# Two units of weights on GpSimd's queue and another order of the head's steps, in linear attention followed by a gated feed-forward layer

## The chip, the cores and the metric

The kernel runs on one core of one Trainium2 chip. The metric is device time in microseconds from launch to end, lower is better. A profiled execution gives besides a span, from the first to the last instruction of the core, and a trace of every engine. TensorE (PE) multiplies; VectorE (DVE), ScalarE (ACT) and GpSimd (POOL) work elementwise; SyncE (SP) issues most of the DMA transfers.

## The reference

There are 8 batches of 8 heads, 576 tokens and head size 64. For each head the kernel computes a small matrix from keys and values, applies it to the queries, and normalises each row. The rows of all heads of one token are then put side by side (512 wide) and go through a feed-forward layer with a sigmoid gate, whose weights come as 64-bit floats:

```python
kv = einsum('bhsd,bhse->bhde', k, v)            # 64 x 64 per head
o  = einsum('bhsd,bhde->bhse', q, kv)
o  = o / sqrt(mean(o*o, axis=-1) + 1e-6) * g_norm
x  = o.transpose(0, 2, 1, 3).reshape(4608, 512)
gate = 1 / (1 + exp(-(x @ w_gate)))             # w_gate, w_val: 512 x 1536
out  = (gate * (x @ w_val)) @ w_out             # w_out: 1536 x 512
```

## The kernel before

The 4608 tokens are worked in nine groups of 512. Group 0 is computed plainly; groups 1 to 8 use products of sums of blocks, a scheme of fast matrix multiplication with 26 products in place of 32. The change touches only the head: the attention of the first two batches (eight pairs of heads, n = 0 to 7), the conversion of the first five units of weights, and the first four blocks of group 0's first layer.

**A pair of heads** goes through eleven steps (`attention`, L265 to L345). KV (TensorE) forms both 64x64 matrices; KVO (DVE) copies them to SBUF and issues the loads of k and v for pair n+4. Q (TensorE) turns the queries; QO (ACT) copies them and issues the load of q for pair n+4. U (TensorE) multiplies the two. SQ (ACT) squares, SUM (DVE) adds up, ROOT (ACT) takes the root, NORM (DVE: a reciprocal and a product) scales. X (TensorE) turns the rows to columns and XO (ACT) copies them to xT, the operand of the feed-forward layer. KV and Q of a pair share one place in PSUM, so KVO waits for both, QO waits for KVO, and the next pair's KV waits for QO. U and X of a pair share another, one for even and one for odd pairs.

**A unit of weights** is 128 columns of w_gate and the same of w_val (2 x 512 KB of 64-bit floats). `load_unit` (L135) loads it with two transfers into one of three staging buffers, and `convert` (L161) makes 32-bit floats from it in five steps on DVE (c0 to c4) with two on ACT between (a0 follows c0, a1 follows c1, c2 waits for a0, c3 for a1). Unit u+3 goes into the buffer that c4 of unit u has freed.

**A block** (`Plain`, L554) is one 128-column piece of both products for group 0: four accumulating matmuls for the gate, four for the value, each over 128 of the 512 inputs and all 512 tokens. Block f needs unit f converted, and matmul m of it needs XO of pair m. Blocks 0 to 2 share two PSUM banks. CG and CV copy a finished block out, G is its sigmoid straight from PSUM, S the sigmoid of a copy, M and E form the product of gate and value.

**The order** is written out by hand as a string of tokens (L594): `KV0` is the step KV of pair 0, `c1.2` step c2 of unit 1, `a1.0` its step a0, `b0.1.3` matmul 3 of the value of block 0, `w2` the loads of unit 2, and `warm10` ten matmuls of the identity that only keep TensorE busy. Each engine runs its own instructions in this order and waits only where an operand or a place needs it. SyncE's queue is in the order in which the program issues loads: k, v and q of pairs 0 and 1, unit 0, pairs 2 and 3 (L231), and then as the tokens come. SyncE has at most eight transfers in flight: each issue waits for the one eight before it.

After the head TensorE goes on with blocks 4 to 11 (`plain`, L573), in which DVE converts the other units step by step. After block 8 the keys and values of batch 2 are multiplied (L366), and then GpSimd begins to form the sums of weights for the fast scheme (L741). Until then it has nothing to do but the identity matrix at the start (`make_identity`, L252).

Of the kernel before, what the change touches and what calls it, by code (L numbers as in the profile page):

```python
# [20 lines left out]
def kernel(  # L21
# [11 lines left out]
    nc = tc.nc  # L33
# [26 lines left out]
    NMT = DM // P  # L60
# [74 lines left out]
    def load_unit(u):  # L135
        if u >= len(units):
            return
        kind, f = units[u]
        staged[u] = st = raw.tile([P, 2, DM], I64, tag="st", name="st", bufs=NST)
        for i in range(2):  # L140
            if kind == "gv":
                src = (moe_w_gate, moe_w_val)[i].rearrange("(m p) f -> p m f", p=P)[:, :, P * f:P * f + P]
                nc.sync.dma_start(out=st[:, i].rearrange("p (m f) -> p m f", m=NMT), in_=src)
            else:
                nc.sync.dma_start(out=st[:, i], in_=moe_w_out[P * (f + i):P * (f + i) + P, :])

# [14 lines left out]
    def convert(u):  # L161
# [45 lines left out]
        def s4():  # L207

            m, p = d["m"], d["p"].bitcast(FP32)
            if kind == "gv":  # L210
                vec.scalar_tensor_tensor(out=m, in0=m, scalar=g_col, in1=p, op0=ALU.mult, op1=ALU.mult)
            else:
                vec.tensor_tensor(out=m, in0=m, in1=p, op=ALU.mult)
            if u > 1:
                load_unit(u + NST)
# [15 lines left out]
    for n in range(4):  # L231
        load_kv(n)
        load_q(n)
        if n == 1:
            load_unit(0)


    w1 = const.tile([P, N3, 4 * NMT, 2, P], FP32, name="w1")
    w2 = const.tile([P, NFT, DM], FP32, name="w2")
# [333 lines left out]
    def plain(c, u, ps):  # L573
# [18 lines left out]


    order = """  # L594
        warm10 KV0 Q0 KVO0 QO0 w1 warm3 U0 SQ0 KV1 SUM0 ROOT0 Q1 KVO1 NORM0 QO1 warm3 U1 SQ1 SUM1 X0 c0.0 c0.1
        XO0 ROOT1 NORM1 warm13 KV2 warm2 Q2 KVO2 a0.0 c0.2 X1 a0.1 c0.3 c0.4 QO2 w2 warm6 U2 SQ2 KV3 Q3 b0.0.0 b0.1.0
        KVO3 XO1 QO3 w3 U3 SUM2 KV4 Q4 ROOT2 NORM2 SQ3 SUM3 ROOT3 X2 XO2 b0.0.1 b0.1.1 b0.0.2 NORM3 X3 KVO4 QO4
        U4 c1.0 a1.0 c1.1 a1.1 c1.2 c1.3 b0.1.2 KV5 Q5 KVO5 XO3 b0.0.3 b0.1.3 SQ4 c1.4 w4 SUM4 QO5 U5 CG0 CV0
        KV6 Q6 b1.0.0 ROOT4 NORM4 X4 b1.1.0 b1.0.1 b1.1.1 SQ5 SUM5 ROOT5 KVO6 QO6 XO4 U6 NORM5 X5 c2.0 c2.1 a2.0
        c2.2 b1.0.2 KV7 Q7 SQ6 SUM6 a2.1 b1.1.2 ROOT6 c2.3 b1.0.3 XO5 b1.1.3 KVO7 QO7 U7 c2.4 NORM6 CG1 X6 CV1  # L600
        b2.0.0 SQ7 XO6 b2.1.0 b2.0.1 c3.0 SUM7 ROOT7 b2.1.1 c3.1 a3.0 a3.1 NORM7 X7 XO7 c3.2 c3.3 c3.4 b2.0.2
        b2.1.2 b2.0.3 c4.0 S0 S1 b2.1.3 M0 G2 M1 b3.0.0 b3.1.0 a4.0 E2 c4.1 a4.1 c4.2 c4.3 b3.0.1 b3.1.1 b3.0.2
        b3.1.2 b3.0.3 b3.1.3 c4.4
    """
    blks, copies = {}, {}
    warm = mm0_ps()
    for token in order.split():
        name = token.rstrip("0123456789.")
        n = [int(i) for i in token[len(name):].split(".")]
        f = n[0]  # L610
# [10 lines left out]
        elif name == "CG":  # L621
            copies[f, 0] = sg_tile()
            nc.scalar.copy(out=copies[f, 0], in_=blks[f].ps[0])
        elif name == "CV":
            copies[f, 1] = sg_tile()
            nc.vector.tensor_copy(out=copies[f, 1], in_=blks[f].ps[1])
        elif name == "S":
            nc.scalar.activation(out=copies[f, 0], in_=copies[f, 0], func=AF.Sigmoid)
        elif name == "M":
            nc.vector.tensor_tensor(out=gv_tile(0, F_ORDER[f]), in0=copies[f, 1], in1=copies[f, 0], op=ALU.mult)  # L630
        elif name == "G":
            blks[f].gate()
        elif name == "E":
            blks[f].end()
        elif name in ("c", "a"):
            conversion[f][name][n[1]]()
        elif name == "w":
            load_unit(f)
        elif name == "warm":
            for _ in range(f):  # L640
                nc.tensor.matmul(warm[:, 0:P], ident, ident, start=True, stop=True)
        else:
            a[f][steps[name]]()
            if token == f"Q{NE - 1}":
                first_ctx.__exit__(None, None, None)
                hp = ctx.enter_context(tc.tile_pool(name="hp", bufs=1))
                h_main = [hp.tile([P, 4 * NT, P], FP32, name=f"h{j}") for j in range(N3)]
                h_more = hp.tile([P, N3, 3 * NT, P], FP32, name="h_more")
# [449 lines left out]
    X1 = (12, 16, 16, 17, 18, 18, 19, 19, 19, 20, 20, 21, 21, 24, 25, 25, 25, 25)  # L1098
    X2 = (14, 15, 16, 17, 19, 21, 24, 25, 25, 25, 25, 25, 25, 25, 25, 25, 25, 25)
    X3 = (7, 8, 11, 11, 12, 13, 14, 14, 16, 16, 19, 22, 22, 22, 22, 22, 23, 23)  # L1100
# [49 lines left out]
```

## Time and profile before

| | |
|---|---|
| time, median of 3 runs | 1019.01 us (1017.05 to 1019.85) |
| profiled execution, its own time | 1019.05 us |
| its span | 1017.3 us |
| TensorE busy | 1005.9 us, 99% of the span |
| DVE, ACT, GpSimd busy | 728.1, 350.2, 602.4 us |
| moved by DMA | 193.89 MB, mean 191 GB/s |
| first weights converted (c4 of unit 0 starts) | 21.45 us |
| first matmul of block 0 starts | 22.85 us |
| keys and values of batch 2 (L366) start on TensorE | 98.34 us |
| first sum on GpSimd (L741) starts | 99.11 us |

Times in the views are in microseconds from the span's start. A line of the timeline gives start, length, engine, source line, operation, output<-input, shape, how many instructions are merged, and in brackets how long the engine was idle before and what released it. TensorE runs a 32-bit matmul in two recorded parts, so a count of 24 is twelve matmuls. A line of windows gives the stretch, the busy time of each engine with its count, the granted clock of TensorE, the mean busy share of the 16 DMA engines and what they moved in GB/s. Issuing a DMA isn't counted as busy.

### The profile page before, as it was taken

The numbers are of one execution on the slowest core, as the hardware profiler recorded it, in microseconds if no ns is written. First come the engines' busy times: TensorE is split into PE (matmuls) and PEld (weight loads), VectorE is DVE, ScalarE is ACT, GpSimd is POOL, SyncE is SP. The second block draws the span as 40 slices with busy tenths as digits, with TensorE's granted clock in tenths as the row PEclk, the third lists the DMA queues.
The fourth block names the chain that finished last, engine by engine and source line by source line (L and its number), as shares of the span: only waits on it lengthen the run. The fifth ranks groups of instructions, "written<-read, shape, count | busy, mean of one in ns | idle before, by whom it ended". The sixth has DMA issues, their size and how long they took to land.

```text
span 1017.3 us, 18352 instructions
## 1 busy us (share of the span) xinstructions
PE 1005.9 (99%) x6914; PEld 827.5 (81%) x6914; DVE 728.1 (72%) x1211; ACT 350.2 (34%) x609; POOL 602.4 (59%) x965
## 2 busy tenths in 40 slices
PE   8999999999999999999999999999999999999998
PEld 7644447888878888888888888888888888888887
DVE  4799899899758846775668666866688466755672
ACT  4654422442144304541254115421553033203320
POOL 0000999998539651867177706952496439743963
PEclk9999999999999999999999999999999999999999
DMA  9975315645876568646675577656765545454614
GB/s 267 272 234 192 124 42 160 217 133 183 273 256 224 164 198 262 232 159 197 210 252 178 164 224 231 211 157 184 239 203 162 186 159 202 162 157 159 208 59 126
DMA packets 101128, 193.89 MB, mean 191 GB/s; under 512 B 27408, under 2 KB 74128, under 8 KB 101040
## 3 DMA queue, kind: packets, MB, share of 16 engines
q0 software_dynamic: 20976, 112.87, 33.1%
q1 hardware_dynamic: 72896, 77.75, 25.1%
q10 hardware_dynamic: 7168, 2.10, 0.9%
q8 instruction: 55, 0.90, 0.4%
q14 instruction: 33, 0.27, 0.1%
HBM read 160.04 MB, written 25.56 MB: 182 GB/s over the span
## 4 chain that ended last, share of the span: by engine, by line
PE 73%; POOL 2%; DMA 1%; issue 0%; DVE 0%; POOLq 0%
PE mm L932 46%; PE mm L1029 24%; PE at L407 2%; POOL h L722 1%; DMA h_more<-in_v_dram 1%; PE at L366 1%; POOL w_ring L1003 0%; POOL h_more L722 0%; PE at L372 0%; POOL w L770 0%; DVE sg L902 0%; POOL w L1003 0%; POOLq L1003 0%
## 5 line engine op out<-in xcount | busy, mean ns | idle before, releaser
L932 PE MATMUL mm<-xs,w 128*128 128x256 f32 x1428 | 331.7, 380 | 0.0
L932 PEld LDWEIGHTS mm<-xs,w 128*128 128x128 f32 x1428 | 270.6, 190 | 37.0
L932 PE MATMUL mm<-xT,w 128*128 128x256 f32 x948 | 230.1, 380 | 0.0
L932 PEld LDWEIGHTS mm<-xT,w 128*128 128x128 f32 x948 | 179.3, 190 | 25.5 <-issue 1.0
L902 DVE TENSOR_TENSOR sg<-sg,mm 128x512 f32<-128x512 f32 (+1 forms) x176 | 100.8, 600 | 95.7 <-PE mm L932 49.9
L770 POOL DMA_DIRECT2D w<-kept x84 | 47.1, 561 | 190.2 <-PE mm L932 188.6
L1029 PE MATMUL mm<-w,h 128*128 128x256 f32 x630 | 143.4, 379 | 1.4 <-POOL h L722 0.9
L1029 PEld LDWEIGHTS mm<-w,h 128*128 128x128 f32 x630 | 119.5, 190 | 18.4 <-POOL h L722 1.3
L898 ACT COPY temps<-mm 128x512 f32<-128x512 f32 (+1 forms) x128 | 66.0, 538 | 189.7 <-PE mm L1029 94.7
L894 POOL TENSOR_TENSOR h<-h,sg 128x512 f32<-128x512 f32 x72 | 97.7, 1373 | 49.8 <-DVE h L902 34.1
L722 POOL TENSOR_TENSOR h<-h 128x128 f32<-128x128 f32 x216 | 115.7, 548 | 16.5 <-DVE h_more L722 13.1
L1029 PE MATMUL mm<-w,h_more 128*128 128x256 f32 x474 | 108.2, 379 | 0.0
L891 ACT ACTIVATE sg<-sg 128x512 f32<-128x512 f32 x96 | 59.7, 630 | 135.0 <-DVE sg L902 135.0
L1029 PEld LDWEIGHTS mm<-w,h_more 128*128 128x128 f32 x474 | 90.1, 190 | 12.2
L898 ACT COPY sg<-mm 128x512 f32<-128x512 f32 (+1 forms) x112 | 57.0, 510 | 90.9 <-PE mm L1029 48.7
L722 POOL TENSOR_TENSOR h_more<-h 128x128 f32<-128x128 f32 x120 | 58.7, 492 | 34.4 <-DVE h L894 30.0
L561 PE MATMUL mm<-xT,w 128*128 128x512 f32 x176 | 77.7, 594 | 0.0
L902 DVE TENSOR_TENSOR temps<-temps,mm 128x512 f32<-128x512 f32 (+1 forms) x96 | 59.3, 618 | 25.6 <-PE mm L1029 17.6
L902 DVE TENSOR_TENSOR temps<-mm,temps 128x512 f32<-128x512 f32 (+1 forms) x64 | 39.8, 622 | 51.2 <-PE mm L1029 23.6
L898 ACT COPY h<-mm 128x512 f32<-128x512 f32 x48 | 28.0, 586 | 128.0 <-PE mm L932 112.5
L741 POOL TENSOR_TENSOR h_more<-w 128x256 f32<-128x256 f32 x10 | 12.9, 1300 | 97.8 <-PE at L366 97.8
L902 DVE TENSOR_TENSOR sg<-mm,sg 128x512 f32<-128x512 f32 (+1 forms) x64 | 39.5, 618 | 39.8 <-PE mm L932 20.7
(132 smaller groups left out, 1325.4 us busy)
## 6 DMA issues: line engine op xcount, KB each, us to landing
w<-kept POOLq DMA_DIRECT2D x42, 896.0 KB, 5.3
w<-kept POOLq DMA_DIRECT2D x90, 384.0 KB, 4.7
w<-kept POOLq DMA_DIRECT2D x42, 768.0 KB, 5.4
q<-in_q_dram SPq DMA_DIRECT2D x24, 288.0 KB, 3.1
out_dram<-sg SPq DMA_DIRECT2D x104, 64.0 KB, 1.7
st<-in_moe_w_gate_dram SPq DMA_DIRECT2D x12, 512.0 KB, 5.0
st<-in_moe_w_val_dram SPq DMA_DIRECT2D x12, 512.0 KB, 6.7
h_more<-in_k_dram SPq DMA_DIRECT2D x24, 256.0 KB, 5.4
```

The costliest lines, as they stand in the source:

```text
L366: nc.tensor.matmul(ps[HD * e:HD * e + HD, n // 2, n % 2], mains[n, "k"][:, c], mains[n, "v"][:, c], start=(n % 2 == 0 and j == 0), stop=Fa ...
L407: nc.tensor.matmul(u[HD * e:HD * e + HD, r, o:o + HD], qTs[QB * r:QB * r + QB, (n0 + which) % 2, c:c + PH], kvq[QB * r:QB * r + QB, (n0 + ...
L561: nc.tensor.matmul(self.ps[i], w[("wg", "wv")[i], self.f][:, m, :], xT[self.c][:, m, :], start=(m == 0), stop=(m == NMT - 1), skip_group_c ...
L722: ops.append((eng, lambda v=v, x=x, sign=sign, y=y, eng=eng: eng.tensor_tensor(out=h_form(v, j), in0=h_form(x, j), in1=h_form(y, j), op=op ...
L741: nc.gpsimd.tensor_tensor(out=w1_slot(j, w_at[v]), in0=w1_slot(j, w_at[x]), in1=w1_slot(j, w_at[y]), op=op_of(sign))
L770: nc.gpsimd.dma_start(out=granule(g)[:, 0:n], in_=kept1[g // NPA % N3, g % NPA][:, 0:n])
L891: nc.scalar.activation(out=o["o" + step[1]], in_=o["o" + step[1]], func=AF.Sigmoid)
L894: mult.tensor_tensor(out=o[x], in0=o[x], in1=o[y], op=ALU.mult)
L898: nc.scalar.copy(out=o[out_], in_=o[expr])
L902: tt(out=o[out_], in0=o[x], in1=o[y], op=ALU.add if sign == "+" else ALU.subtract)
L932: nc.tensor.matmul(regions[name][1][:, g], ws[:, g], xf[c][wv], start=(new and g == 0), stop=True, skip_group_check=True)
L1029: nc.tensor.matmul(regions[name][1], h_form(hv, j), ws[:, j], start=(used[i] and j == 0), stop=(j == N3 - 1), skip_group_check=True)
```

## The change

Units 0 and 1 are loaded by GpSimd's queue, the others by SyncE's as before. The order of the head's tokens is another; the set of steps is the same but for the warm-ups (`warm`), which are 20 instead of 37. `w1` stands among the tokens of pair 1 (before: of pair 0), `w3` and `w4` to a later place behind `SQ6`; `S0` and `M0` move to the end, behind block 3.

```diff
@@ -140,7 +140,7 @@
         for i in range(2):
             if kind == "gv":
                 src = (moe_w_gate, moe_w_val)[i].rearrange("(m p) f -> p m f", p=P)[:, :, P * f:P * f + P]
-                nc.sync.dma_start(out=st[:, i].rearrange("p (m f) -> p m f", m=NMT), in_=src)
+                (nc.gpsimd if u < 2 else nc.sync).dma_start(out=st[:, i].rearrange("p (m f) -> p m f", m=NMT), in_=src)
             else:
                 nc.sync.dma_start(out=st[:, i], in_=moe_w_out[P * (f + i):P * (f + i) + P, :])
 
@@ -592,15 +592,15 @@
 
 
     order = """
-        warm10 KV0 Q0 KVO0 QO0 w1 warm3 U0 SQ0 KV1 SUM0 ROOT0 Q1 KVO1 NORM0 QO1 warm3 U1 SQ1 SUM1 X0 c0.0 c0.1
-        XO0 ROOT1 NORM1 warm13 KV2 warm2 Q2 KVO2 a0.0 c0.2 X1 a0.1 c0.3 c0.4 QO2 w2 warm6 U2 SQ2 KV3 Q3 b0.0.0 b0.1.0
-        KVO3 XO1 QO3 w3 U3 SUM2 KV4 Q4 ROOT2 NORM2 SQ3 SUM3 ROOT3 X2 XO2 b0.0.1 b0.1.1 b0.0.2 NORM3 X3 KVO4 QO4
-        U4 c1.0 a1.0 c1.1 a1.1 c1.2 c1.3 b0.1.2 KV5 Q5 KVO5 XO3 b0.0.3 b0.1.3 SQ4 c1.4 w4 SUM4 QO5 U5 CG0 CV0
-        KV6 Q6 b1.0.0 ROOT4 NORM4 X4 b1.1.0 b1.0.1 b1.1.1 SQ5 SUM5 ROOT5 KVO6 QO6 XO4 U6 NORM5 X5 c2.0 c2.1 a2.0
-        c2.2 b1.0.2 KV7 Q7 SQ6 SUM6 a2.1 b1.1.2 ROOT6 c2.3 b1.0.3 XO5 b1.1.3 KVO7 QO7 U7 c2.4 NORM6 CG1 X6 CV1
-        b2.0.0 SQ7 XO6 b2.1.0 b2.0.1 c3.0 SUM7 ROOT7 b2.1.1 c3.1 a3.0 a3.1 NORM7 X7 XO7 c3.2 c3.3 c3.4 b2.0.2
-        b2.1.2 b2.0.3 c4.0 S0 S1 b2.1.3 M0 G2 M1 b3.0.0 b3.1.0 a4.0 E2 c4.1 a4.1 c4.2 c4.3 b3.0.1 b3.1.1 b3.0.2
-        b3.1.2 b3.0.3 b3.1.3 c4.4
+        warm6 KV0 Q0 warm1 KVO0 QO0 U0 SQ0 SUM0 c0.0 c0.1 warm4 ROOT0 NORM0 KV1 Q1 KVO1 a0.0 X0 w1 QO1 U1 KV2
+        Q2 warm5 SQ1 SUM1 ROOT1 KVO2 NORM1 c0.2 X1 XO0 a0.1 c0.3 QO2 c0.4 warm3 w2 warm1 U2 SQ2 XO1 KV3 Q3
+        KVO3 b0.0.0 b0.1.0 QO3 U3 SUM2 ROOT2 KV4 c1.0 NORM2 X2 SQ3 Q4 SUM3 b0.0.1 XO2 b0.0.2 KVO4 ROOT3 b0.1.1
+        a1.0 NORM3 X3 c1.1 c1.2 QO4 KV5 a1.1 c1.3 Q5 KVO5 XO3 U4 SQ4 b0.0.3 QO5 b0.1.2 U5 c1.4 SUM4 b0.1.3
+        ROOT4 NORM4 SQ5 KV6 SUM5 CV0 CG0 X4 ROOT5 XO4 Q6 KVO6 b1.1.0 b1.1.1 c2.0 QO6 a2.0 U6 SQ6 w3 w4 KV7
+        NORM5 Q7 c2.1 b1.0.0 b1.1.2 b1.0.1 b1.0.2 KVO7 a2.1 SUM6 ROOT6 c2.2 X5 XO5 b1.0.3 QO7 c2.3 b1.1.3 c2.4
+        NORM6 U7 CG1 CV1 c3.0 SQ7 SUM7 c3.1 a3.0 b2.1.0 ROOT7 X6 a3.1 b2.0.0 XO6 c4.0 b2.1.1 S1 b2.0.1 b2.0.2
+        b2.0.3 G2 c3.2 NORM7 c3.3 c3.4 c4.1 M1 X7 XO7 b2.1.2 b2.1.3 b3.0.0 b3.1.0 E2 a4.0 c4.2 a4.1 c4.3
+        b3.0.1 b3.1.1 b3.0.2 b3.1.2 b3.0.3 b3.1.3 S0 M0 c4.4
     """
     blks, copies = {}, {}
     warm = mm0_ps()
```

## The prediction

> **What bounds the kernel now.** I read the chain that ended last first, then the waits, then the head in windows and in order of time. The chain (by engine) is TensorE with a little GpSimd:
>
> ```profile
> PE 73%; POOL 2%; DMA 1%; issue 0%; DVE 0%; POOLq 0%
> ```
>
> GpSimd's part ends at 261 us, where TensorE waits for it; and GpSimd itself was started by TensorE (waits of the whole run; engine and line, for whom, us, times, longest):
>
> ```profile
> POOL h_more L741 <- PE at L366: 97.8, 1, 97.8
> PE mm L1029 <- POOL h L722: 0.9, 1, 0.9
> ```
>
> So a shift of TensorE's stream before 98 us goes through both to the end. Where the stream is made up is the head, up to block 3 (`b3.0.0`). Windows (us, busy of PE, PEld, DVE, ACT, POOL, clock, DMA share, GB/s):
>
> ```profile
> 0.00:5.00 5.00, 3.63 (x18) 3.63 (x18) 0.12 (x3) 1.49 (x2) 0.70 (x6) 1.00 0.56 154
> 5.00:10.00 5.00, 4.53 (x107) 3.98 (x106) 0.63 (x2) 1.34 (x2) 0.00 (x0) 1.00 1.11 314
> 10.00:15.00 5.00, 4.71 (x77) 4.45 (x76) 2.86 (x6) 2.67 (x7) 0.00 (x0) 1.00 1.12 298
> 15.00:20.00 5.00, 4.07 (x55) 3.84 (x54) 2.96 (x6) 2.83 (x3) 0.00 (x0) 1.00 1.04 267
> 20.00:25.00 5.00, 5.00 (x99) 3.51 (x102) 4.25 (x7) 2.30 (x6) 0.00 (x0) 1.00 1.05 304
> 70.00:75.00 5.00, 5.00 (x13) 2.21 (x12) 4.43 (x5) 2.03 (x3) 0.00 (x0) 1.00 1.09 377
> ```
>
> The DMA engines are full (share over 1) from 5 us on, with one queue issuing: nearly all of it SyncE's. From 20 us on TensorE never pauses. Order of time, TensorE and DVE around the point where it starts to run without pause:
>
> ```profile
> 14.64 0.70 DVE L179 TENSOR_SCALAR w<-st 128x1024 uint32<-128x1024 uint32 x1 [0.71 <-DMA st<-in_moe_w_val_dram]
> 16.83 0.92 PE L276 MATMUL two<-v,k 96*64 96x64 f32 x24 [0.93 <-DMA v<-in_v_dram]
> 18.23 0.66 PE L287 MATMUL two<-ident,q 96*128 96x96 f32 x6
> 18.73 0.71 PE L333 MATMUL two<-ident,sqs 128*128 128x128 f32 x5
> 19.27 1.50 PE L641 MATMUL mm<-ident 128*128 128x128 f32 x12
> 20.71 0.81 PE L306 MATMUL two<-kvq,qTs 64*64 64x64 f32 x40
> ```
>
> TensorE waits for the third pair's v until 16.83, DVE for unit 0 until 14.64. `b0.0.0` starts at 22.85. From there to `b3.0.0` lie 24 matmuls of 128x512 (0.861 each, 20.7), five U (0.74), four KV (0.85), four Q (0.55) and six X (0.55): 33.3 us of work in 34.2 us, since `b3.0.0` follows at 57.06 (X7 ends at 53.62, then four of 0.861). So the head is: wait for data to 16.83, six more us of steps, then 34.2 us of full TensorE.
>
> **What the Trainium skill says.** "DMA: Bandwidth & Descriptors", section "Issuing engines are not separate DMA queues": transfers issued by any engine run on the same 16 DMA engines and interleave; a second issuer saves only issue time. The trace agrees as far as it goes: one queue alone holds the share above 1. The same page, "Queues, rings and completion order": each DMA engine goes round robin between queues, packet by packet; so two full queues share. No stretch of this trace has both full with these packets. The same page, "Specifications": GpSimd's path has its first byte after about 1 us, SyncE's after about 0.6 us; too little to matter here. "TensorE: Matmul & The Clock Gate", Part 1: TensorE starts at half clock and reaches full clock after some 3.4 us of work. The trace agrees: the first ten warm-ups take 4.13 us (0.41 each), the thirteen from 12.84 on 3.07 us (0.236 each).
>
> **The change, part by part.**
>
> *Units 0 and 1 on GpSimd's queue.* The order of instructions in the changed kernel shows them at GpSimd's start: unit 0, then the identity, then unit 1. None of these waits for anything (GpSimd's next waiting instruction is the sum of 98 us). Unit 1, issued at 19 us before, now starts at about 3 us. SyncE's queue keeps its order, without these four transfers. It has eight transfers in flight (each issue waits for the one eight back), so taking out two issues of 0.6 us frees no time while the DMA engines are full.
>
> Bytes: k or v of a pair 96x2x384x4 = 0.295 MB, q 0.295, a unit 1.049. When v2 had landed at 16.83, the windows had moved 0.77+1.57+1.49+0.49 = 4.32 MB; ahead of and with v2 stand six k/v, two q and one unit, 3.41 MB; so 0.91 MB behind it had moved too. In the new kernel the step that takes v2's place as the anchor is Q2 (q of the third pair): six k/v, three q and two units, 4.75, plus the same 0.91: 5.66 MB. 0.77 of it is moved by 5 us, 4.89 remain. At 306 GB/s (mean of 5 to 15 us, the stretch with the same mixture) 16.0 us: Q2 starts at 21.0, where before it was 18.23. Bounds: at 377 GB/s (the highest window) 13.0, so 18.0; at 267 (the lowest of the head) 18.3, so 23.3.
>
> *Identity behind unit 0's descriptors.* Nearest row: a GpSimd DMA issue of 128 rows takes 0.56 us; these have 512 rows. Between 2x0.56 and 2x4x0.56 the identity comes 1.1 to 4.5 us after 1.31 (its end before), six cold warm-ups (2.5) follow, so KV0 could start at 4.9 to 8.3. Its data, sharing the engines with unit 0, comes at about 6.5, and Q0's at 9 (6.28 before). Nothing is lost at either end; without that cover, up to 3 us on KV0.
>
> *Other order up to b0.0.0.* 17 warm-ups fewer (37 to 20), 17x0.236 = 4.0 us of TensorE. Before, 13 of them stand ahead of the wait that ended at 16.83, so they were free; the rest covered QO and NORM. I take nothing for them. From Q2 on in the new order: Q2 0.55, warm5 1.2, X1 (after KVO2, reciprocal and NORM1 on DVE: 2.05 after Q2's start, a wait of 0.3), X1 0.55, four warm-ups 0.95, U2 0.74, KV3 0.85, Q3 0.55: 5.7. DVE has KVO2, NORM1, then c0.2 1.14, c0.3 1.15, c0.4 1.28: done 5.7 after Q2 as well. So `b0.0.0` starts 5.8 after Q2: 26.8, against 22.85. KV3 and Q3 need 0.88 MB more than Q2, 2.9 us, and come 4.3 us after it: covered.
>
> *Order from b0.0.0 to b3.0.0.* The same matmuls; I find no new pause. X2 now waits for NORM2 behind c1.0, which reads unit 1: landed by then (full share for GpSimd puts it near 16). XO7 stands behind the table load (1.28), S1 and G2 on ACT, but has two matmuls (1.7) before `b3.0.0` and frees its banks in time. S0 and M0 move behind; M0 (0.65) comes before c4.4, whose slack to block 4 was 63.95-63.21 = 0.7 before. Between these, 0 to +0.7 us; I take 0.
>
> *Units 2 to 7.* On SyncE they keep their places among the loads; unit 2 landed about 2 us ahead of c2.0 before and both move together: nothing.
>
> Sum: +3.95 us at b0.0.0, carried through 34.2 us of full TensorE, the dense blocks to 98 us, GpSimd's start there, and the end. The profiled execution was 1019.05 (span 1017.3, 1.75 around it), 0.04 above the median of 1019.01. 1019.05 + 3.95 = 1023.0.
>
> **Rivals.**
>
> *Two queues move more than one.* The gaps between transfers of one queue are filled. Speaks for it: windows of 366 to 377 GB/s exist where only 1 KB rows move. Against: the head's q has 256 B rows, and share is full already. At 340 to 377 GB/s Q2 is at 19.4 to 18.0, b0.0.0 at 25.2 to 23.8: +2.3 to +0.9, about 1020.8.
>
> *Not slower: the pairs go ahead of unit 1, and only the steps bound.* If SyncE's queue gets most of the engines and unit 1 is served last, 3.84 MB instead of 4.89 stand ahead of Q2. Decided at Q2 = 17.05 (22.85 less 5.8): 3.84 MB in 12.05 us, 319 GB/s, while unit 0 still lands in time. Its floor without any wait for data: KV0 at 5.1, U0 2.6 later, NORM0 5.2 after it (with c0.0 and c0.1 in between, 1.2), then X0, KVO1, QO1, U1, KV2 to Q2 at about 15.5; b0.0.0 at 21.2, -1.6: 1017.4. So 17 warm-ups fewer can't make it faster by 3 us.
>
> *GpSimd's queue is starved.* If SyncE's packets get four fifths, unit 0 moves at about 60 GB/s and lands at 20 to 21; c0.0 holds DVE, behind it NORM0, KVO1 and all later pairs. From c0.0 at 21.2, b0.0.0 comes 11 us later (NORM0 +2.3, QO1 and KV2, Q2 +4.9, then 5.8): 32.2, +9.3; unit 1 holds NORM2 again. 1028 to 1034.
>
> *Cold clock.* With six warm-ups and pauses of one or two us the array may be at half clock when b0 starts: at most 3.4 us at half speed, +1.7 on top.
>
> **How the numbers follow.** Main case (equal sharing, 267 to 330 GB/s, +2.7 to +6.2; its own range 1021.7 to 1025.3) 0.52; two queues move more 0.26; not slower 0.09; starved 0.08; cold clock on top 0.05. No change that can be told from noise is within 0.3%, 3.06 us. Faster needs more than the floor gives, and only something unseen does it: 0.04. Same: the second and third case and the lower edge of the first, 0.37. Slower 0.59. Range: below 1018.5 only the best part of the third case, above 1030 the worse half of starvation.
>
> **What would show it.** Right: KV1, Q1 and Q2 wait for DMA, Q2 starts near 21, `b0.0.0` near 27, the sums on GpSimd begin near 103 instead of 99.11, GB/s about 300 from 5 to 20 us. Wrong: Q2 before 18 with over 340 GB/s; c0.0 waiting for unit 0 beyond 15; 128x512 matmuls over 0.861 at b0; or new pauses between b0 and b3.

## The result, and the profile after

The changed kernel takes 1028.08 us (1028.04 to 1028.69) against 1019.01: a ratio of 1.0095, 95% interval 1.0071 to 1.0118. It is slower by 9.1 us, where +4.0 was forecast. Its profiled execution took 1028.69 us, with a span of 1026.9 (before: 1019.05 and 1017.3), so the traces have 9.6 us to explain.

The chain by engine looks as before:

```profile
PE 72%; POOL 2%; DMA 1%; issue 0%; SPq 0%; DVE 0%; POOLq 0%
```

The waits of the whole run (engine and line, for whom, us, times, longest):

```profile
POOL h_more L741 <- PE at L366: 104.8, 1, 104.8
PE mm L1029 <- POOL h L722: 0.9, 1, 0.9
PE at L366 <- DMA h_more<-in_v_dram: 0.6, 1, 0.6
```

GpSimd still waits for TensorE and TensorE for GpSimd once, so a shift made in the head goes to the end, as the prediction had it. The shift is larger than thought. Windows of the head (us, busy of PE, PEld, DVE, ACT, POOL, clock, DMA share, GB/s):

```profile
0.00:5.00 5.00, 1.44 (x7) 1.44 (x7) 0.12 (x3) 1.49 (x2) 3.83 (x10) 1.00 0.49 108
5.00:10.00 5.00, 2.53 (x31) 2.16 (x30) 0.00 (x0) 0.00 (x0) 0.00 (x0) 1.00 0.95 293
10.00:15.00 5.00, 0.00 (x0) 0.00 (x0) 0.00 (x0) 0.00 (x0) 0.00 (x0) 0.53 1.09 291
15.00:20.00 5.00, 3.88 (x52) 3.50 (x53) 0.28 (x2) 1.34 (x2) 0.00 (x0) 0.50 1.14 266
20.00:25.00 5.00, 5.00 (x49) 4.33 (x51) 3.14 (x6) 2.09 (x3) 0.00 (x0) 0.50 1.08 269
```

From 10 to 15 us no engine does anything, while the DMA engines are full and move 291 GB/s: the wrong bytes arrive. The clock column stands at about half from 10 to 25 us. TensorE in order of time, before:

```profile
6.28 0.71 PE L287 MATMUL two<-ident,q 96*128 96x96 f32 x6
...
22.85 1.93 PE L561 MATMUL mm<-xT,w 128*128 128x512 f32 x4
```

and after:

```profile
6.42 1.11 PE L276 MATMUL two<-v,k 96*64 96x64 f32 x24
15.61 1.19 PE L287 MATMUL two<-ident,q 96*128 96x96 f32 x6 [8.09 <-DMA q<-in_q_dram]
...
21.08 1.55 PE L276 MATMUL two<-v,k 96*64 96x64 f32 x24
...
27.47 0.71 PE L287 MATMUL two<-ident,q 96*128 96x96 f32 x6
...
33.28 1.91 PE L561 MATMUL mm<-xT,w 128*128 128x512 f32 x4
```

Q0, which started at 6.28 before, waits 8.09 us for its q. From Q0 to Q2 it is 11.86 us (before 11.95), from Q2 to `b0.0.0` 5.81 (before 4.62). So of the 10.43 us by which `b0.0.0` is late, 9.33 are Q0's. That Q0 to Q2 takes the same time twice is chance: before, the stretch holds thirteen warm-ups and a wait for v of the third pair; after, it holds no wait for data, but its steps are long. KV1 takes 1.55 us in place of 0.92. "Cold" stands below for these long durations, "warm" for the short ones.

What arrived in place of q shows in the DMA view of 5 to 15 us, by queue: packets, MB, and the time that the packets took as a share of 16 engines. q0 is GpSimd's queue, q1 SyncE's; "software" and "hardware" are the profile's words for the two kinds. Before:

```profile
q1 hardware_dynamic: 4654, 3.05, 110.7%
```

and after:

```profile
DMA packets 2376, 2.92 MB, mean 292 GB/s; under 512 B 1553, under 2 KB 1864, under 8 KB 2376
q0 software_dynamic: 576, 2.10, 63.6%
q1 hardware_dynamic: 1720, 0.82, 37.9%
```

GpSimd's queue moves units 0 and 1 complete, 2.10 MB. 512 packets of the view are over 2 KB (2376 less 1864), so these hold it all, at 4 KB each; the other 64 of its 576 packets hold next to nothing. SyncE's queue moves 1720 packets, mostly under 512 bytes: these are q's rows of 256 bytes. It gets three times the packets and 28% of the bytes. At the worst, from 10 to 12 us:

```profile
q0 software_dynamic: 181, 0.66, 94.6%
q1 hardware_dynamic: 180, 0.05, 11.7%
```

This is one for one. From 6 to 9 us, while GpSimd's packets filled 77% of the engines' time and not yet 94%, SyncE's queue still got three packets for one (614 to 210). The Trainium skill says in "DMA: Bandwidth & Descriptors", "Queues, rings and completion order", that turns go by packet, and in "SWDGE vs HWDGE vs iDMA" that a packet of GpSimd's path is preferably no larger than 4096 bytes. The trace agrees with both; the prediction quoted the first and then shared the time equally.

### The profile page after: what moved, and what is told of

It is laid out like the page before. It is cut to its first block, busy times and chain, and to the rows that moved or that the text cites. A ratio compares the mean times of both kernels' runs of the same rounds, so it can differ in the third digit from the quotient of the medians.

```text
span 1026.9 us, 18289 instructions
## 1 busy us (share of the span) xinstructions
PE 1007.1 (98%) x6880; PEld 827.9 (81%) x6880; DVE 728.6 (71%) x1211; ACT 349.8 (34%) x609; POOL 603.7 (59%) x969
## 4 chain that ended last, share of the span: by engine, by line
PE 72%; POOL 2%; DMA 1%; issue 0%; SPq 0%; DVE 0%; POOLq 0%
PE mm L932 45%; PE mm L1029 24%; PE at L407 2%; POOL h L722 1%; DMA h_more<-in_v_dram 1%; PE at L366 1%; POOL w_ring L1003 0%; SPq L118 0%; POOL h_more L722 0%; PE at L372 0%; POOL w L770 0%; DVE sg L902 0%; POOL w L1003 0%; POOLq L1003 0%
## 5 line engine op out<-in xcount | busy, mean ns | idle before, releaser
L932 PE MATMUL mm<-xs,w 128*128 128x256 f32 x1428 | 331.9, 380 | 0.9 <-issue 0.9
L932 PEld LDWEIGHTS mm<-xs,w 128*128 128x128 f32 x1428 | 270.5, 190 | 38.3 <-issue 1.3
L932 PE MATMUL mm<-xT,w 128*128 128x256 f32 x948 | 230.1, 380 | 0.0
L932 PEld LDWEIGHTS mm<-xT,w 128*128 128x128 f32 x948 | 179.3, 190 | 25.5 <-issue 1.1
```

The costliest lines, as they stand in the source:

```text
L932: nc.tensor.matmul(regions[name][1][:, g], ws[:, g], xf[c][wv], start=(new and g == 0), stop=True, skip_group_check=True)
```

## The experiments

The theory from the trace, "packets": two full queues take turns packet by packet, so a queue of 256-byte packets beside one of 4 KB packets gets next to nothing, Q0 is late, and TensorE loses its clock while it waits. The rivals: the new order costs something by itself; GpSimd's path or the late identity does; any second queue does.

To compare the traces, the span's difference from before is split at three marks of TensorE: the start of `b0.0.0` (22.85 before), of L366 for batch 2 (98.34) and of L366 for batch 4 (398.12). "Time" is the difference of medians to the kernel before on the same chip.

| kernel | Q0 | to b0.0.0 | to L366 | to batch 4 | to the end | span | time | ratio (interval) |
|---|---|---|---|---|---|---|---|---|
| changed | 15.61 | +10.4 | +0.2 | -0.4 | -0.6 | +9.6 | +9.1 | 1.0095 (1.0071 to 1.0118) |
| e1 old order, GpSimd | 15.56 | +9.8 | 0.0 | -0.6 | -0.6 | +8.7 | +8.8 | 1.0089 (1.0065 to 1.0112) |
| e2 new order, SyncE | 6.73 | +4.3 | +3.1 | +0.3 | -0.3 | +7.3 | +6.9 | 1.0068 (1.0046 to 1.0090) |
| e3 gate | 6.66 | +6.9 | +0.2 | +2.4 | -0.6 | +9.0 | +9.6 | 1.0102 (1.0075 to 1.0129) |
| e4 wide q rows | 11.29 | +6.5 | +0.2 | -2.4 | +0.2 | +4.4 | +6.4 | 1.0067 (1.0040 to 1.0094) |
| e5 26 warm-ups | 15.45 | +7.9 | +0.2 | -0.5 | +1.5 | +9.1 | +10.4 | 1.0108 (1.0091 to 1.0125) |
| e6 ScalarE's queue | 11.07 | +5.9 | +4.2 | -1.3 | -0.3 | +8.4 | +4.6 | 1.0048 (1.0028 to 1.0068) |
| e7 c steps back | 6.29 | +2.8 | +1.1 | -0.6 | -0.4 | +2.9 | +4.6 | 1.0041 (1.0027 to 1.0055) |
| e8 unit 0 only | 12.03 | +5.6 | +1.7 | -0.5 | -0.2 | +6.6 | +7.0 | 1.0072 (1.0057 to 1.0087) |
| e9 c steps and a0.0 back | 7.25 | +2.3 | +1.5 | -0.8 | +0.1 | +3.1 | +1.9 | 1.0021 (1.0013 to 1.0029) |
| e10 20 warm-ups | 15.06 | +8.5 | +0.2 | +1.1 | -0.4 | +9.5 | +8.9 | 1.0081 (1.0063 to 1.0100) |
| e11 before, wide q rows | 7.85 | +4.3 | +0.3 | -2.4 | -0.2 | +2.0 | +3.1 | 1.0031 (1.0018 to 1.0045) |
| e12 as e9, ten warm-ups | 6.23 | +2.8 | +1.3 | +2.0 | 0.0 | +6.1 | +6.2 | 1.0062 (1.0042 to 1.0081) |

### e1: the queue alone

The kernel before, with its order, and one line of the change:

```diff
-                nc.sync.dma_start(out=st[:, i].rearrange("p (m f) -> p m f", m=NMT), in_=src)
+                (nc.gpsimd if u < 2 else nc.sync).dma_start(out=st[:, i].rearrange("p (m f) -> p m f", m=NMT), in_=src)
```

> The old order of steps, units 0 and 1 on GpSimd's queue. Packets theory (GpSimd's 4096-byte packets take turns with the 256-byte packets of q, so q of pair 0 is held up until both units are through, and all steps after it are late): Q0 near 15 us as in the changed kernel, b0.0.0 at 31 to 34, time 1027 to 1031. Bytes theory (two units more ahead of the pairs, in fair shares): Q0 near 9, b0.0.0 at 27 to 29, 1023 to 1025. Order theory (the new order alone is to blame): b0.0.0 at 23, 1019.

Measured: 1027.62 us. TensorE:

```profile
15.56 1.19 PE L287 MATMUL two<-ident,q 96*128 96x96 f32 x6 [7.17 <-DMA q<-in_q_dram]
```

The DMA view of 5 to 15 us has 572 packets (2.08 MB) on GpSimd's queue and 1833 (0.89 MB) on SyncE's; from 10 to 12 us it has 178 on each. In the old order the one line of the queue alone gives nearly the whole loss, as the packets theory had it.

### e2: the order alone

The changed kernel, with its order, and that line undone:

```diff
-                (nc.gpsimd if u < 2 else nc.sync).dma_start(out=st[:, i].rearrange("p (m f) -> p m f", m=NMT), in_=src)
+                nc.sync.dma_start(out=st[:, i].rearrange("p (m f) -> p m f", m=NMT), in_=src)
```

> The new order of steps, all units on SyncE's queue. Packets theory: Q0 back at 6.3, Q2 near 18 behind the wait for v of pair 2, b0.0.0 at 24 to 25; unit 1, now late in SyncE's queue, may hold c1.0 and NORM2 by up to 3 us; time 1020 to 1024. Bytes theory: b0.0.0 at 23 to 25, the same range. Order theory: b0.0.0 over 30, 1027 or more.

Measured: 1025.70 us, more than the packets theory allowed. Q0 is on time, but TensorE waits at X0 and later at X2:

```profile
16.91 1.30 PE L333 MATMUL two<-ident,sqs 128*128 128x128 f32 x5 [3.70 <-DVE kvq L280]
33.44 0.77 PE L333 MATMUL two<-ident,sqs 128*128 128x128 f32 x5 [2.29 <-DVE sqs L325]
```

The cause is on DVE, in order of time:

```profile
14.41 0.69 DVE L179 TENSOR_SCALAR w<-st 128x1024 uint32<-128x1024 uint32 x1 [3.04 <-DMA st<-in_moe_w_val_dram]
15.02 0.69 DVE L190 TENSOR_SCALAR cz<-st 128x1024 uint32<-128x1024 uint32 x1
15.62 0.21 DVE L323 RECIPROCAL ms<-ms 128x10 f32<-128x10 f32 x1
...
31.71 0.69 DVE L179 TENSOR_SCALAR w<-st 128x1024 uint32<-128x1024 uint32 x1 [3.44 <-DMA st<-in_moe_w_val_dram]
```

In the new order c0.0 and c0.1 stand in front of NORM0, and c1.0 in front of NORM2. With the units on SyncE's queue they wait 3.04 and 3.44 us for weights, and the norms behind them too. So the order needs the early units, and the early units spoil Q0. The two losses don't add up (8.7 and 7.3 alone, 9.6 together): with Q0 at 15.6 the weights have landed before DVE asks, and in the changed kernel c0.0 starts at 20.68 with no wait for them.

### e3: the units behind q of pair 0

The changed kernel, with the identity made first and then a copy of one column of pair 0's q on GpSimd, ahead of the issue of unit 0, so that both units wait for q (the lines that made the identity later are left out here):

```diff
+            ident = const.tile([P, P], FP32, name="ident")
+            make_identity(nc, ident)
+            gate = const.tile([NP, 2], FP32, name="gate")
+            for e in range(2):
+                nc.gpsimd.tensor_copy(out=gate[:, e:e + 1], in_=pairs[0]["q"][:, 0, e, 0:1])
...
```

> The changed kernel, but the identity is made first and GpSimd reads one column of q of pair 0 before it issues unit 0, so both units start after q of pair 0 has landed. Packets theory: Q0 near 6.3; now q of pair 1 is held up behind the two units, Q1 at 14 to 17 instead of 22.6; b0.0.0 at 25 to 28 instead of 33.3; time 1020 to 1024. Bytes theory: the same bytes stand ahead of Q2, b0.0.0 at 27, 1023. Order theory: b0.0.0 over 30, 1027 or more.

Measured: 1028.35 us; Q0 6.66 as the packets theory wanted, but `b0.0.0` is 1.8 us and the time over 4 us beyond its ranges. The time is in the range of the order theory, though `b0.0.0` isn't. From 5 to 12 us SyncE's queue moves 1.72 MB in 2999 packets, nearly alone (GpSimd's has 26 packets, at the end of the stretch); GpSimd's 576 packets go between 11 and 21 us. Then unit 0 is late for its place in the order:

```profile
17.41 0.69 DVE L179 TENSOR_SCALAR w<-st 128x1024 uint32<-128x1024 uint32 x1 [5.56 <-DMA st<-in_moe_w_val_dram]
```

X0 waits 5.47 us behind it and `b0.0.0` comes at 29.77, 3.5 us earlier than in the changed kernel. That gain is lost again later ("to batch 4", +2.4; see below). The gate shows that the late Q0 is the queue's doing and not the new order's. It doesn't mend the kernel: with Q0 on time, units that come late still leave `b0.0.0` 6.9 us behind.

### e4: q's rows made wide

The changed kernel, with q of pairs 0 and 1 loaded as rows of 1536 bytes, in one transfer for two, and turned by half matmuls:

```diff
+            if n < 2:
+                wide = t.rearrange("p j e d -> p (j e d)").rearrange("p (e c) -> p e c", e=2)
+                nc.sync.dma_start(out=wide, in_=q[b, h0:h0 + 2].rearrange("h (p j) d -> p h (j d)", j=NJ))
...
+                    for e in range(2):
+                        nc.tensor.matmul(ps[HD * e:HD * e + HD, j // JH, c0:c0 + NP],
+                                         pairs[n]["wide"][:, e, HD * j:HD * j + HD], ident[0:NP, 0:NP],
+                                         start=True, stop=True)
```

> The changed kernel, but q of pairs 0 and 1 is loaded in rows of 1536 bytes instead of 256, and each of its six transposes is done as two half ones (identity matmuls), 0.4 us more for Q0 and for Q1. Packets theory: six times larger packets hold their own against GpSimd's; Q0 at 9 to 11 instead of 15.6, b0.0.0 at 25 to 29, time 1020 to 1025. Bytes theory and order theory: bytes and order are the same, so b0.0.0 stays at 33 to 34 and the time at 1028.

Measured: 1025.20 us. TensorE and the DMA view of 5 to 15 us:

```profile
11.29 2.19 PE L294 MATMUL two<-ident,q 96*64 96x96 f32 x24 [3.31 <-DMA q<-in_q_dram]
```

```profile
q0 software_dynamic: 523, 1.94, 63.7%
q1 hardware_dynamic: 622, 0.89, 32.5%
```

With the same bytes in 1536-byte rows TensorE waits 3.31 us for q in place of 8.09, though Q0 and Q1 got dearer on TensorE (2.19 and 1.44 us for 1.19 and 1.22). Q0, `b0.0.0` (29.30) and the time each lie just beyond the late end of the packets theory's ranges, and far from those of the others. From 10 to 15 us the two queues take turns one for one:

```profile
q0 software_dynamic: 312, 1.14, 72.5%
q1 hardware_dynamic: 313, 0.44, 31.8%
```

SyncE's queue now gets 28% of the bytes of a stretch in which both are busy, where it got 7% with 256-byte rows from 10 to 12 us. A second queue that starves the first whatever its packets is out. Besides the packet of q, only the number of its transfers and the way q is turned differ. So the size of q's packets is worth 4.3 of the 9.3 us by which Q0 is late; the other 5.0 remain while 1536-byte packets take turns with 4 KB ones.

### e5 and e10: the clock during the wait

The changed kernel with the wait for Q0 filled; this is e5, and e10 has `warm20` at the same place:

```diff
-        warm6 KV0 Q0 warm1 KVO0 QO0 U0 SQ0 SUM0 c0.0 c0.1 warm4 ROOT0 NORM0 KV1 Q1 KVO1 a0.0 X0 w1 QO1 U1 KV2
+        warm6 KV0 warm26 Q0 warm1 KVO0 QO0 U0 SQ0 SUM0 c0.0 c0.1 warm4 ROOT0 NORM0 KV1 Q1 KVO1 a0.0 X0 w1 QO1 U1 KV2
```

> The changed kernel with 26 more warm-ups between KV0 and Q0, which fill TensorE's wait for q of pair 0; nothing else differs. Packets and a cold clock (the late Q0 delays the head, and the wait itself drops TensorE to half clock, which stretches the steps after it): Q0 still starts at 15.3 to 16.3 us, the granted clock is 0.8 to 1.0 from 10 to 25 us in place of 0.50 to 0.53, b0.0.0 comes 1.5 to 3 us earlier than 33.28, at 30.3 to 31.8, and the time is 1025 to 1026.8. Rival, the clock doesn't matter because DVE and the transfers set the pace of the steps: b0.0.0 within 0.7 us of 33.28, time 1027.4 to 1028.7.

> As the kernel with 26 more warm-ups, but with 20: the wait for q of pair 0 is filled down to 2.5 to 3.2 us, and TensorE's later instructions stand 6 warm-ups earlier in its stream. If the clock is all that they change: b0.0.0 at 30.3 to 31.5, L366 at 106 to 107, and 2 us less than the changed kernel to the end, 1025.5 to 1026.5; the 1029.5 with 26 was then chance. If TensorE's pauses without a releaser (1.0 us at L407 and 0.3 us at L932 with 26, 0.9 us at L932 in the changed kernel) go with an instruction's place in the stream: such pauses at other instructions than with 26, and a time anywhere from 1025.5 to 1030.

Measured: 1029.54 us with 26 and 1027.52 with 20. In e5, in order of time:

```profile
15.45 0.69 PE L287 MATMUL two<-ident,q 96*128 96x96 f32 x6 [1.55 <-DMA q<-in_q_dram]
...
24.62 0.71 PE L287 MATMUL two<-ident,q 96*128 96x96 f32 x6
...
30.76 1.91 PE L561 MATMUL mm<-xT,w 128*128 128x512 f32 x4
```

From Q0 to Q2 it is now 9.17 us in place of 11.86, and `b0.0.0` comes 2.5 us earlier. The clock column still reads 0.79 and 0.87 from 15 to 25 us, so this is what the cold clock costs at `b0.0.0` at the least. The Trainium skill, "TensorE: Matmul & The Clock Gate", Part 1, has the clock at half after an idle window of about 3.4 us. The wait was 8.09 us in the changed kernel. In e10 one of 2.31 us, behind twenty warm-ups that took 0.24 us each, was enough:

```profile
15.06 1.19 PE L287 MATMUL two<-ident,q 96*128 96x96 f32 x6 [2.31 <-DMA q<-in_q_dram]
```

That is shorter than the page's figure. But the time didn't fall with 26. At L366 e5 is 2.5 us ahead of the changed kernel; it loses 1.5 us behind batch 4, most of it in two pauses of 1.00 and 0.29 us (see below), and its other executions lie up to 2.3 us above the profiled one. The clock is shown as a term of the head; that it is worth 2.5 us of the time is not.

### e6: another queue, smaller packets

```diff
-                (nc.gpsimd if u < 2 else nc.sync).dma_start(out=st[:, i].rearrange("p (m f) -> p m f", m=NMT), in_=src)
+                (nc.scalar if u < 2 else nc.sync).dma_start(out=st[:, i].rearrange("p (m f) -> p m f", m=NMT), in_=src)
```

> The changed kernel with units 0 and 1 on ScalarE's queue in place of GpSimd's, so that (as on SyncE's queue) each packet should be a row of 1 KB and not 4 KB. Turns by packet: a packet of q of pair 0 (256 bytes) waits for one of 1 KB, not of 4 KB, so q0's 0.295 MB have some 1.2 MB of weights beside them, 1.5 MB in all, 5 us at 300 GB/s; Q0 starts at 10 to 12.5 us in place of 15.61, b0.0.0 at 27 to 30, time 1021.5 to 1025. Rival, a second full queue starves the first whatever its packets: Q0 at 14.5 or later, b0.0.0 at 32 to 34.5, time 1026.8 to 1029. Equal shares by bytes: Q0 at 8 to 9.5, time 1020 to 1022.

Measured: 1023.73 us, Q0 at 11.07, `b0.0.0` at 28.71, all inside the ranges of turns by packet. The DMA view of 5 to 12 us (q10 is ScalarE's queue):

```profile
q1 hardware_dynamic: 2488, 1.30, 78.8%
q10 hardware_dynamic: 736, 0.57, 35.4%
```

This doesn't show what smaller packets are worth, because more than the packet differs. Unit 1 is issued only at 16.86 us, behind other steps of ScalarE, so up to 12 us half the weights stand beside the pairs (1.05 MB), as in e8 below, where Q0 comes at 12.03. They also begin earlier, and even KV0 waits:

```profile
8.06 1.55 PE L276 MATMUL two<-v,k 96*64 96x64 f32 x24 [3.77 <-DMA v<-in_v_dram]
```

Of SyncE's 1.30 MB, 0.94 go after 8.5 us, when ScalarE's queue has 0.01 MB left. The profiled execution was the slowest of e6's (1027.44 us): it has a pause of 2.21 us in U that ends at 43.40, with the clock column at 0.82 and 0.83 up to 50 us, which is most of the +4.2 in its row.

### e8: half the load

```diff
-                (nc.gpsimd if u < 2 else nc.sync).dma_start(out=st[:, i].rearrange("p (m f) -> p m f", m=NMT), in_=src)
+                (nc.gpsimd if u < 1 else nc.sync).dma_start(out=st[:, i].rearrange("p (m f) -> p m f", m=NMT), in_=src)
```

> The changed kernel with only unit 0 on GpSimd's queue, unit 1 on SyncE's where w1 stands. Turns by packet: the 256 large packets of unit 0 are through by 9 to 10 us, and q of pair 0 right after; Q0 at 10 to 12.5 us, b0.0.0 at 26 to 29; unit 1 then comes late, and c1.0 ahead of NORM2 makes X2 wait 1 to 3 us; time 1022 to 1026. Rival, the identity behind unit 0's descriptors or GpSimd's issue is what delays Q0: Q0 at 14.5 or later, time 1027 to 1030.

Measured: 1026.16 us. Q0 comes at 12.03 and `b0.0.0` at 28.49; X2 waits 0.88 us. This is what turns by packet gave, with the time just beyond its range. With the same start of GpSimd (first warm-up at 3.57 in place of 3.56) and half of its packets, Q0 is 3.6 us earlier: the amount of large packets sets it, not the identity or the time of an issue. Between `b0.0.0` and L366 it loses 1.7 us; X2's wait behind c1.0 for unit 1, on SyncE's queue again, is the part of it that the trace shows, beside a pause of 0.32.

### e7, e9 and e12: what the order costs

```diff
-        warm6 KV0 Q0 warm1 KVO0 QO0 U0 SQ0 SUM0 c0.0 c0.1 warm4 ROOT0 NORM0 KV1 Q1 KVO1 a0.0 X0 w1 QO1 U1 KV2
+        warm6 KV0 Q0 warm1 KVO0 QO0 U0 SQ0 SUM0 warm4 ROOT0 NORM0 KV1 Q1 KVO1 c0.0 c0.1 a0.0 X0 w1 QO1 U1 KV2
...
-        KVO3 b0.0.0 b0.1.0 QO3 U3 SUM2 ROOT2 KV4 c1.0 NORM2 X2 SQ3 Q4 SUM3 b0.0.1 XO2 b0.0.2 KVO4 ROOT3 b0.1.1
-        a1.0 NORM3 X3 c1.1 c1.2 QO4 KV5 a1.1 c1.3 Q5 KVO5 XO3 U4 SQ4 b0.0.3 QO5 b0.1.2 U5 c1.4 SUM4 b0.1.3
+        KVO3 b0.0.0 b0.1.0 QO3 U3 SUM2 ROOT2 KV4 NORM2 X2 SQ3 Q4 SUM3 b0.0.1 XO2 b0.0.2 KVO4 ROOT3 b0.1.1
+        NORM3 X3 c1.0 a1.0 c1.1 c1.2 QO4 KV5 a1.1 c1.3 Q5 KVO5 XO3 U4 SQ4 b0.0.3 QO5 b0.1.2 U5 c1.4 SUM4 b0.1.3
```

This is e7. e9 is e7 with `a0.0` taken from behind `c0.1` to behind `ROOT1`, and e12 is e9 with `warm10` in place of the `warm6` at the start. All three load every unit on SyncE's queue, as e2 does.

> The new order with every unit on SyncE's queue, and the conversion's steps c0.0 and c0.1 moved back behind KVO1, c1.0 behind NORM3. Order theory (what the new order costs by itself is that c0.0 and c1.0 stand on DVE ahead of NORM0 and NORM2 and wait for weights): X0 no longer waits over 1 us, Q2 starts at 18 to 19.5 us in place of 20.89, b0.0.0 at 23.5 to 25.5 in place of 27.11, X2 no longer waits 2.3 us, time 1019 to 1021.5. Rival, the missing warm-ups and the half clock: clock still 0.5 in 15 to 20 us, b0.0.0 at 26 or later, time 1023.5 to 1026.

> The kernel of the experiment before (new order, all units on SyncE's queue, c0.0, c0.1 and c1.0 moved back) with the step a0.0 on ScalarE moved back too, behind ROOT1; there it stood ahead of QO1 and waited 3.63 us for c0.0. Order theory (three steps of the conversion set too early are the whole cost of the new order): U1 starts by 13.5 us in place of 16.09, the third pair waits for its data only, Q2 at 17.3 to 18.8, b0.0.0 at 23 to 24.7, keys and values of batch 2 (L366) at 98.5 to 100.3, time 1018.5 to 1021. Rival, the 17 missing warm-ups and with them a cold clock cost something of their own: clock at half in 15 to 20 us, b0.0.0 at 25 or later, time 1021.5 to 1024.

> The kernel of the last experiment on the order (new order, all units on SyncE's queue, three steps of the conversion moved back) with ten warm-ups ahead of KV0, as before, in place of six. There KV0, Q0, U0, KV1, Q1, X0 and U1 all ran at the long duration (KV 1.55 us, U 1.35) up to 19 us. If the missing warm-ups are what is left of the loss: KV0 and the steps after it at 0.92 and 0.81, U1 by 14 us in place of 16.41, Q2 at 17.5 to 18.6, b0.0.0 at 23 to 24.2 in place of 25.17, time 1018 to 1019.8, no difference from before to be told. Rival, the rest of the loss lies in the later order: short durations, but b0.0.0 to L366 longer than before's 75.5 us, L366 at 99.5 or later, time 1020 to 1021.5.

e7, 1023.75 us: X0 no longer waits long (0.71 us), but U1 does, 3.29 us. The time and the clock from 15 to 20 us (0.51) are as the rival of the cold clock had them, but the cold comes behind U1's wait, and ScalarE shows what made that:

```profile
14.36 1.15 ACT L184 ACTIVATE w<-w,one 128x1024 f32<-128x1024 uint32 x1 [3.63 <-DVE w L179]
15.42 0.62 ACT L292 COPY qTs<-two 128x576 f32<-128x576 f32 x1
```

QO1 (L292) stands behind a0.0 (L184), which waits for c0.0, which waits for the weights. e9 moves a0.0 too: 1020.58 us, ratio 1.0021. So 5 of the 7 us that the new order costs by itself are steps of the conversion set in front of steps of the pairs, on two engines. The rest didn't come as expected. U1 was to start by 13.5 us and started at 16.41, in an execution of 1022.20 us, slower than most of e9's. From KV1 on nothing waited; the steps were long:

```profile
5.10 1.55 PE L276 MATMUL two<-v,k 96*64 96x64 f32 x24 [0.81 <-DMA v<-in_v_dram]
...
12.71 1.55 PE L276 MATMUL two<-v,k 96*64 96x64 f32 x24
14.19 1.22 PE L287 MATMUL two<-ident,q 96*128 96x96 f32 x6
...
16.41 1.35 PE L306 MATMUL two<-kvq,qTs 64*64 64x64 f32 x40
```

Six warm-ups had left the array cold here, as in e3 and e4; in e2 and e7 it was warm at KV0 behind the same six. e12 puts ten there, as before, and KV0 runs at 0.92 and U1 starts at 12.71. Yet `b0.0.0` comes at 25.64, later than in e9, and the time is 1025.85:

```profile
12.71 0.81 PE L306 MATMUL two<-kvq,qTs 64*64 64x64 f32 x40
17.79 1.55 PE L276 MATMUL two<-v,k 96*64 96x64 f32 x24 [4.27 <-DMA v<-in_v_dram]
```

Now TensorE is early and waits 4.27 us for v of pair 2, idle, and is cold behind it. Before, thirteen warm-ups stood at exactly this wait, which left 0.93 us of it, and KV2 took 0.92. So those warm-ups seem to be no padding, though no run puts them into e12. U1 and KV0 were as expected of the warm-ups, but the time lies above both ranges; the +2.0 "to batch 4" is treated below.

### e11: wide rows without a second queue

The edit of e4, for pairs 0 to 3, on the kernel before.

> The kernel before with the q rows of pairs 0 to 3 loaded as 1536 bytes in place of 256, and their turning done by half matmuls (twice as many for Q0 to Q3); the output is the same. Packets theory: with one queue there is nobody to take turns with, and the gain is only what short rows cost by themselves: v2 lands at 15.5 to 16.8 us in place of 16.83, Q0 to Q3 cost 0.5 to 0.9 us more each, b0.0.0 at 22 to 24, time 1017.5 to 1020.5. Rival, short rows slow the DMA engines as such, not only in turns: v2 by 14 us, b0.0.0 before 21.5, time 1015 to 1017.

Measured: 1021.69 us, slower than before by 0.3%. `b0.0.0` comes at 27.12. From 5 to 10 us the DMA engines moved 255 GB/s (before 314), so wide rows bring nothing by themselves, and Q0 to Q3 cost 1.2 us each. v2, issued at 6.90 and 10.3 us on the way, landed at 17.2 (before 16.7), later than either theory said; why is open. KV2 didn't wait for it but started at 19.54: TensorE got there late, behind the dearer Q0 and Q1, a wait of 1.25 us for q of pair 0 and a pause of 1.23 us among its warm-ups. No kernel of the table is faster than the kernel before.

## Where the times and the heads part

"To b0.0.0" explains the order of most rows, but not e3, e5, e10 and e12. Two places of the later kernel vary. One is TensorE's wait for v of batch 3 at its second L366, 2.18 us in the kernel before:

```profile
292.00 0.69 PE L366 MATMUL at<-h_more 128*64 128x64 f32 x16 [2.18 <-DMA h_more<-in_v_dram]
```

It is 0.57 in the changed kernel, nothing in e4 and e11 (their -2.4), and 2.12 in e3. The other is a pause of TensorE for which the view names no releaser. In the changed kernel:

```profile
313.38 4.15 PE L932 MATMUL mm<-xs,w 128*128 128x256 f32 x18 [0.91 <-issue]
```

and in e12:

```profile
306.94 0.33 PE L407 MATMUL at<-kvq,qTs 32*64 32x64 f32 x5 [1.62 <-issue]
```

The kernel before and e1, with the old order, have none behind the head. The kernels with the new order and 20 warm-ups, e4 apart, have one of 0.42 to 1.1 us at the same line (L932; L935 in e3). With 26 warm-ups more it goes to 419 us (1.00, L407), with 20 more there is none up to 470 us, and in e12, with four more, it is at 307. After a wait or a pause the clock can drop: 0.66 from 300 to 305 us in e3, 0.67 in e10, 0.81 and 0.85 from 305 to 315 in e12. So the stretch from L366 of batch 2 to that of batch 4 takes between 297.4 us (e4, e11) and 302.2 (e3) for the same work.

The DMA records show what the pauses go with. Now and then a 16 KB packet comes on a queue of its own, which the profile calls "instruction" (54 or 55 a run); in the changed kernel the view of 310 to 312 us has one:

```profile
q8 instruction: 1, 0.02, 3.3%
```

It runs from 310.76 to 311.81, and TensorE goes on at 313.38. In all 16 pauses without a releaser that the timelines show, in eleven of the fourteen kernels, TensorE goes on 1.2 to 1.6 us after the end of such a packet (e12: packet to 305.68, on at 306.94). By chance one pause in fifty would fall so, since these stretches make up 2% of a run. So TensorE most likely waits there for its own next instructions, which would explain why the pauses move when instructions are added far ahead. No run tests it, and why most such packets come without a pause is open. What is left of the misfit of e3, e5, e10 and e12 stays open beyond that.

## Why the prediction was right or wrong

**Units 0 and 1 on GpSimd's queue (Q2's data at 21.0).** The sum of bytes held: 292 GB/s from 5 to 15 us, against 306 assumed, and the lower bound was 267. Even the arrival held: the two loads of the third pair's q, issued at 14.69 and 15.49, landed at 21.3 and 21.8. What failed is that this anchor binds. The new kernel's Q2 waits for no data; it starts at 27.47, 11.86 us after Q0.

**Identity behind unit 0's descriptors.** KV0 between 4.9 and 8.3: it was 6.42. The first byte "after about 1 us" was not met: GpSimd issued unit 0 at 1.27, and its queue has no packet before 5 us; SyncE issued its first load at 0.74 and has packets before 2 us. The next half sentence is the step that failed: Q0's data "at 9" and "Nothing is lost at either end". It came at 15.61. Equal sharing of two full queues was an assumption by time; the turns go by packets (e1, e4, e8), and from 6 to 12 us SyncE's queue got 0.22 MB beside 1.76. In the sum, 21.0 in place of 18.23 at Q2 (+2.77) should have been +9.33 at Q0. From there the stretch to Q2 has no wait for data and, with most of the cold gone, takes 9.17 us in place of 11.95 (e5: -2.8); the cold clock gives 2.7 back, the order behind Q2 adds 1.2, and that makes 10.4.

**Other order up to `b0.0.0`.** From Q2 on 5.8 was said and 5.81 measured. For 17 warm-ups fewer it took nothing. That can't be relied on: with six ahead of KV0 the array was cold from there on in e9 and warm in e2 and e7, and behind the wait of KV2 it was cold in e12 without the thirteen. In the changed kernel itself the late Q0 hides this; the cold clock adds at least 2.5 us there (e5). That the order puts c0.0 in front of NORM0 was seen only in the rival of a starved GpSimd, and was not priced for weights that come at the old time: 3.0 us on DVE and, behind a0.0, 3.6 on ScalarE (e2, e7).

**From `b0.0.0` to the end.** 0 to +0.7 was said for the later order: +0.2. "Carried to the end" held to about a microsecond: +10.6 at L366 became +9.6 in the span, mostly because the wait of 2.18 us for batch 3 shrank to 0.57 and a pause of 0.91 came in.

**Units 2 to 7.** Nothing, as said.

**The rivals.** Two queues that move more: no, 292 GB/s. Pairs ahead of unit 1: the opposite. GpSimd's queue starved named the right time (1028 to 1034) and the right mechanism with the roles exchanged: SyncE's queue starved. The cold clock came true, though not at `b0.0.0` as put there but from Q0 to Q2, and at 2.5 us or more, not 1.7. The forecast of slower was right, but by another way than the main case's: 1028.08 lies outside its own range (1021.7 to 1025.3) and inside the whole range only by the room left for the rivals, which is partly luck. The size was off by 5 us, in the main for the one step above.

## What to carry to other kernels

Before a second queue is put beside a first, compare the packets of both and not only their bytes: here the one with rows of 256 bytes got 0.22 of 1.98 MB in six us beside packets of 4 KB. Look for what the critical path needs first in those microseconds, and keep large loads off until it is there. And when steps are reordered, look on every engine at what is queued behind a step that waits for data; warm-ups that stand at such a wait can hold the clock.

## What was not expected of the hardware

- Turns by packet are visible to the count: 181 packets of GpSimd's queue and 180 of SyncE's from 10 to 12 us, 0.66 MB and 0.05 MB. The same 1 KB rows of weights went as 4 KB packets on GpSimd's queue (512 for 2.10 MB) and as packets of 1 KB on ScalarE's (the page of e6 has 2112 packets and 2.10 MB more there than before).
- The clock column and the durations can disagree. In e9 the windows from 5 to 20 us show 1.00, and KV takes 1.52 or 1.55 us and U 1.35 up to 19 us, with TensorE busy 5.00 of 5.00 us from 10 to 20. The duration of a known step is the better sign.
- Six warm-ups (2.93 us) ahead of KV0 and then 0.65 to 0.81 us of waiting left KV0 at 0.92 us in e2 and e7 and at 1.55 in e9: the same start can come out either way. e9's executions spread from 1019.05 to 1023.87 us.
- A pause of TensorE of 0.2 to 2.2 us with no releaser in the profile appears and moves when instructions are added far ahead of it. All 16 end 1.2 to 1.6 us behind a 16 KB packet of the queue called "instruction".
